# Block transposes on VectorE and swapped key-value sums in a Performer attention and ELU layer kernel

## The chip, the cores and the metric

The kernel runs on one core of one Trainium2 chip. The metric is device time in microseconds (us): the median of three runs of the whole program, one launch, inputs and output in DRAM. Five engines work side by side and meet through semaphores: TensorE (PE; its weight loads are the row PEld), VectorE (DVE), ScalarE (ACT), GpSimd (POOL) and SyncE (SP), which issues all the DMAs.

## The reference

Attention with random features for 8 batches of 8 heads, 576 tokens, head size 64, 128 features; then a two-layer perceptron with ELU over all 4608 tokens.

```python
# q, k, v: (8, 8, 576, 64); omega: (128, 64); m = 128
def phi(x):                                    # x scaled by 64 ** -0.25
    proj = einsum('bhsd,md->bhsm', x, omega)
    h = proj - sum(x * x, -1, keepdims=True) / 2
    return exp(h - max(h, -1, keepdims=True)) / sqrt(m)
q_p, k_p = phi(q_s), phi(k_s)
kv  = einsum('bhsm,bhsd->bhmd', k_p, v)
z   = sum(k_p, axis=2)
num = einsum('bhsm,bhmd->bhsd', q_p, kv)
den = einsum('bhsm,bhm->bhs', q_p, z)[..., None] + 1e-06
x   = (num / den), heads joined                # (4608, 512)
h   = x @ w_in                                 # w_in: (512, 2048), float64
out = elu(h) @ w_out                           # w_out: (2048, 512), float64
```

## The kernel before

**Tiles.** Two heads of a batch make a pair; there are 32 pairs, four to a batch, numbered i = 0 to 31. The 576 tokens of each head are cut into blocks of 128 rows; the last 64 tokens of both heads share a block, so a pair has nine blocks j of 128 tokens by 128 features. Block 2t + a is tile t of head a, and block 8 holds head 0 in rows 0 to 63 and head 1 in rows 64 to 127. The perceptron runs over 12 blocks of 384 tokens, each in 16 steps of 128 hidden units. One step of `layer1` makes 12 matmuls of 384 columns (lines 764 to 766, three for each of four chunks, because every float32 factor is split into a high and a low float32r part), then ELU on ACT and DVE. One step of `layer2` makes nine matmuls of 512 columns (lines 798 to 800) into three accumulators.

**One pair's attention.** `project` makes `hk` and `hq` (line 488 in float32r, line 437 in the first pairs; the exponentials are line 404). `kv` (lines 530 and 535) sums k_p v and the key sums over the nine blocks: the weights are a block of `hk`, 128 by 128, and the moving operand is `v` with a column of ones, 65 columns, in float32. DVE copies the key sums to `z`, ACT copies the rest to `kvf`, features on partitions. `finish` spreads `z` over all partitions with two transposes on PE (`pz`, line 570). DVE multiplies it with q_p and sums to `den` (line 586), takes the reciprocal (595), and POOL or DVE scales q_p by it. PE then transposes the nine blocks of q_p (`pt`, line 607) into three banks, ACT or DVE copies them to `qh`, and four float32 matmuls (`pn`, line 634) multiply by `kvf`: 64 weight columns each, head 0 to partitions 0 to 63 and head 1 to 64 to 127. The result is split into `xh` (helper line 331 or 333) and `xl` (line 647), the input of `layer1`, kept in a ring of two batches.

**What sets the order.** `op` records each operation with engine, cost, due time and buffers; `order` plays the program through by those costs and takes on every engine, among the operations whose inputs and buffers are there, the one due first. The instructions are issued in that order and each engine runs its own list in order. A buffer class (tag) has a fixed number of slots and a line, sorted by due time. The first in line may take a free slot. Another may do so only for the tags in `LOOSE`, `pa` and `h`, and only while two are free. PSUM has eight banks: three of `pa` (projections, `pkv`, `pz`, `pt` and `pn` of pair 4 on), two of `ph` (the output of `layer1`, and `pkv` and `pz` of the first four pairs) and the three accumulators. A pair's due times are its own time less a constant: for pairs 8 on, loads 56.0, k 46.17, `kv` 30.64, q 29.89, the spread 12.0, the transposes 5, `pn` 2 (lines 53 to 68). Steps of `layer1` are due at `step[F]` (from `MLP0 = 58`, `SEG = [8.62, 6.25, 4.29, 5.37, 3.5, 5.81]` for the first six segments of eight steps, then 16 steps a block at `STEP_ATT = 6.59` beside attention or `STEP = 4.91` without; lines 44 to 47), those of `layer2` 3.5 x 4.91 later. Times of a batch come from the stretch of the segment that it runs beside.

Of the kernel before, what the change touches and what calls it, by code (L numbers as in the profile page):

```python
# [18 lines left out]
P = 128  # L19
# [51 lines left out]

NWARM = 7
# [9 lines left out]
class Buf:  # L82


    def __init__(self, pool, shape, dtype, tag, name, n):
        self.args, self.key, self.n = (pool, shape, dtype, name), tag, n
        self.tile, self.left, self.slot, self.listed = None, 0, None, False
# [8 lines left out]
class Plan:  # L96
# [19 lines left out]
    def op(self, eng, ns, due, fn, reads=(), writes=(), nbytes=0, alt=None):  # L116
# [20 lines left out]
        for b in bufs:  # L137
            b.left += 1
        self.tasks.append((engs, due, f, deps, bufs, nbytes))

    def order(self):
# [51 lines left out]
        while len(done) < len(tasks):  # L193
            started = False
            for eng, q in queue.items():
# [3 lines left out]
                for n in q:  # L199
                    engs, due, _, _, bufs, _ = tasks[n]  # L200
                    if ready[n][eng] > now or (best is not None and due >= first):
                        continue
                    if len(engs) > 1 and not mine(n, eng):
                        continue
                    for b in bufs:
                        if b.slot is None:
                            s = sum(z <= now for z in slots[b.key])
                            if s < (1 if line[b.key][-1] is b else 2 if b.key in self.LOOSE else 99):
                                break
                    else:  # L210
                        best, first = n, due
# [70 lines left out]
def performer_elu_kernel(  # L282
# [33 lines left out]

    kvs = [const.tile([P, P], F32, name=f"kvf{i}") for i in range(2)]

# [3 lines left out]
    part = dram.tile([3 * TB, DM], F32, name="part")  # L322
    xh = const.tile([P, NC, RING], F32R, name="xh")
# [196 lines left out]

    def kv(i, due):

        s = st[i]
# [32 lines left out]
        )  # L556

    def finish(i, due):

        s = st[i]  # L560
        h, z = s["hq"], s["z"]
# [6 lines left out]
        def spread():  # L568
            for a in range(2):
                nc.tensor.transpose(pz()[:, a * P:(a + 1) * P], z()[:, a:a + 1].to_broadcast([P, P]), ident)  # L570

        op("PE", 220, due - DUE_Z, spread, (z,), (pz,))
        qh = Buf(sb, [P, 2, S], F32, "qh", f"qh_{i}", 2)
        for g in range(3):
# [27 lines left out]
            )  # L602
            p = bank(i, "pa", f"pt_{i}_{g}")
# [20 lines left out]
            )  # L624
        kvf = kvs[i % 2]
# [12 lines left out]
        for half, (qs, n, p) in enumerate(halves):  # L638
            xs = slice(qs.start + (b % 2) * S, qs.stop + (b % 2) * S)
            key = (b % 2, hp, half)  # L640
            op(
                "ACT", act(n, True), d + 0.8 + half, lambda e, xs=xs, n=n, p=p: copy(e, xh[:, hp, xs], p()[:, 0:n]),
                (p,), (("xh", key),), alt=other("x_hi", "DVE", dve(n)),
# [6 lines left out]
                (p, ("xh", key)), (("xl", key),),  # L650
# [90 lines left out]
    def ring(blk):  # L741
# [3 lines left out]
        for b in range(2):  # L745
            for half, (s0, n) in enumerate(((0, 256), (256, S - 256))):
                if o < b * S + s0 + n and b * S + s0 < o + TB:
                    keys += [(b, hp, half) for hp in range(NHP)]
# [201 lines left out]
```

## Time and profile before

| | |
|---|---|
| three runs | 1087.62 us median (1086.78 to 1089.88) |
| profiled execution, first to last instruction | 1090.7 us; the page gives no other time for it |
| PE busy | 1060.6 us (97%), weight loads 936.8 us (86%) |
| ACT, DVE, POOL busy | 724.7 (66%), 635.9 (58%), 404.4 (37%) |
| DMA | 176.90 MB, 162 GB/s |
| pairs 0 to 7 (unchanged) | attention from 0 to about 150 us |
| pairs 8 to 31 (changed) | from about 260 us, last `pn` at 945 us |

In rows of groups, the numbers after the bar are the time in which at least one of them ran, the mean length of one, and the idle time of the engine before them. Matmuls overlap, so the length of one is no cost: the cost on PE is the distance from its start to the start of the next. A float32 matmul leaves two MATMUL records, a float32r matmul one. In rows of the order of time come start, length, engine, line, operation, output and inputs, tile, shape and how many were merged.

### The profile page before, as it was taken

The page shows a single profiled execution, that of the slowest core. Times are in us where ns is not written, and L with a number is a line of the kernel's source. Part 1 is how long each engine was busy: PE and PEld are TensorE (multiplying, and loading weights), DVE is VectorE, ACT ScalarE, POOL GpSimd, SP SyncE. Part 2 cuts the span into 40 slices and gives each one's busy share as a digit, 9 for nine tenths or more (in the row PEclk, how much of TensorE's full clock was granted, in tenths as well). Part 3 has the DMA queues.
Part 4 walks back from the last instruction along what each step waited for, and adds up shares of the span by engine and source line. Part 5 has one row for each costly group of instructions (what it writes and reads, how often), then busy time and mean ns, then how long its engine had stood idle before and what let it go on. Part 6 is the DMA issues. An engine that isn't in the chain of part 4 may idle for free.

```text
span 1090.7 us, 19072 instructions
## 1 busy us (share of the span) xinstructions
PE 1060.6 (97%) x5971; PEld 936.8 (86%) x5971; DVE 635.9 (58%) x2403; ACT 724.7 (66%) x2027; POOL 404.4 (37%) x372
## 2 busy tenths in 40 slices
PE   7979888999999999999999999999999999999998
PEld 7867777889988888999888888899888888899987
DVE  6788988775776775225676666324566775322221
ACT  6878774546988986337888988326888888432222
POOL 3568746661223343222343233322233342222221
PEclk8889998999999999999999999999999999999999
DMA  7554656656663554434554645434444452343431
GB/s 213 171 181 161 208 188 240 218 186 205 207 205 130 169 170 150 165 118 157 176 155 153 193 139 170 162 119 150 162 155 167 157 164 79 117 164 119 161 121 63
DMA packets 53235, 176.90 MB, mean 162 GB/s; under 512 B 6032, under 2 KB 6224, under 8 KB 53136
## 3 DMA queue, kind: packets, MB, share of 16 engines
q1 hardware_dynamic: 53136, 175.69, 48.4%
q8 instruction: 48, 0.79, 0.3%
q14 instruction: 51, 0.42, 0.1%
HBM read 155.48 MB, written 20.19 MB: 161 GB/s over the span
## 4 chain that ended last, share of the span: by engine, by line
PE 79%; DVE 9%; ACT 6%; issue 3%; DMA 1%; POOL 1%; SPq 0%; DVEq 0%; POOLq 0%; ACTq 0%
PE ph L764 11%; PE acc L798 10%; PE acc L800 10%; PE ph L766 10%; PE acc L799 10%; PE ph L765 10%; PE pkv L535 4%; PE ppq L488 3%; PE pn L634 3%; PE pt L607 2%; PE ppk L488 2%; ACT hk L404 1%; DVE u_w L697 1%; DVE u_w L704 1%; DVE u_w L709 1%
## 5 line engine op out<-in xcount | busy, mean ns | idle before, releaser
L336 POOL TENSOR_TENSOR g<-e,g 128x384 fp32r<-128x384 f32 x182 | 189.2, 1040 | 547.7 <-DVE g L333 405.9
L764 PE MATMUL ph<-xh,w1c 128*128 128x384 f32 x768 | 267.5, 348 | 6.7 <-DVE e L777 6.2
L766 PE MATMUL ph<-xh,w1c 128*128 128x384 f32 x768 | 259.8, 338 | 0.0
L765 PE MATMUL ph<-xl,w1c 128*128 128x384 f32 x768 | 259.7, 338 | 0.0
L777 DVE SCALAR_TENSOR_TENSOR e<-e,ph 128x384 f32<-128x384 f32 x192 | 105.9, 552 | 237.2 <-ACT e L774 232.8
L798 PE MATMUL acc<-w2h,g 128*128 128x512 f32 x576 | 231.4, 402 | 0.0
L773 ACT ACTIVATE e<-ph 128x384 f32<-128x384 f32 x192 | 93.6, 488 | 206.4 <-PE ph L766 198.4
L800 PE MATMUL acc<-w2h,g 128*128 128x512 f32 x576 | 227.7, 395 | 0.0
L799 PE MATMUL acc<-w2l,g 128*128 128x512 f32 x576 | 227.4, 395 | 0.0
L764 PEld LDWEIGHTS ph<-xh,w1c 128*128 128x128 f32 x768 | 145.6, 190 | 20.1 <-DVE e L777 8.5
L765 PEld LDWEIGHTS ph<-xl,w1c 128*128 128x128 f32 x768 | 145.8, 190 | 7.2
L766 PEld LDWEIGHTS ph<-xh,w1c 128*128 128x128 f32 x768 | 145.4, 189 | 0.3 <-POOL w1c L336 0.3
L800 PEld LDWEIGHTS acc<-w2h,g 128*128 128x128 f32 x576 | 108.5, 188 | 25.5
L798 PEld LDWEIGHTS acc<-w2h,g 128*128 128x128 f32 x576 | 108.7, 189 | 15.1 <-issue 2.3
L799 PEld LDWEIGHTS acc<-w2l,g 128*128 128x128 f32 x576 | 108.8, 189 | 12.2
L336 POOL TENSOR_TENSOR hq<-hq,den 128x512 f32<-128x512 f32 (+1 forms) x96 | 90.4, 961 | 36.1 <-DVE den L595 24.6
L774 ACT ACTIVATE e<-e 128x384 f32<-128x384 f32 x192 | 100.7, 525 | 3.1
L333 DVE CAST g<-e 128x384 fp32r<-128x384 f32 x166 | 72.8, 439 | 23.5 <-PE acc L800 18.8
L586 DVE CUSTOM_DVE_ANT_0 junk<-hq,pz 128x128 f32<-128x128 f32 (+1 forms) x320 | 74.1, 279 | 16.9 <-PE pz L570 16.1
L506 DVE CUSTOM_DVE_ANT_0 hq<-ppq,p2q 128x128 f32<-128x128 f32 x216 | 54.3, 287 | 41.8 <-ACT p2q L497 40.2
L506 DVE CUSTOM_DVE_ANT_0 hk<-ppk,p2k 128x128 f32<-128x128 f32 x225 | 56.5, 286 | 36.1 <-ACT p2k L497 34.3
L497 ACT ACTIVATE p2q<-ppq,sqq 128x128 f32<-128x128 f32 x216 | 67.8, 367 | 12.5 <-PE ppq L488 10.8
(82 smaller groups left out, 1620.3 us busy)
## 6 DMA issues: line engine op xcount, KB each, us to landing
w1c<-w1s SPq DMA_DIRECT2D x176, 512.0 KB, 3.3
raw_w<-in_w_dram SPq DMA_DIRECT2D x32, 512.0 KB, 3.6
xk<-in_kx_dram SPq DMA_DIRECT2D x25, 576.0 KB, 3.9
xq<-in_qx_dram SPq DMA_DIRECT2D x24, 576.0 KB, 4.6
v<-in_v_dram SPq DMA_DIRECT2D x32, 325.0 KB, 3.4
out_dram<-o SPq DMA_DIRECT2D x36, 256.0 KB, 2.9
w1s<-w1c SPq DMA_DIRECT2D x16, 512.0 KB, 3.2
xq<-in_q_dram SPq DMA_DIRECT2D x8, 288.0 KB, 4.0
```

What stands on the lines that cost most here:

```text
L336: (nc.vector if e == "DVE" else nc.gpsimd).tensor_tensor(*args)
L506: nc.vector.tensor_tensor_reduce(out=h()[:, j, :], in0=view()[:, a, 0:M], in1=p2()[:, a, :], scale=1.0, scalar=LOWEST, op0=ALU.subtract, o ...
L586: nc.vector.tensor_tensor_reduce(out=junk()[r], in0=h()[r, j, :], in1=pz()[r, a * P:(a + 1) * P], scale=1.0, scalar=EPS, op0=ALU.mult, op1 ...
L764: nc.tensor.matmul(ph(), wh, xh[:, c, o:o + TB], start=(c == 0), stop=False)
L765: nc.tensor.matmul(ph(), wh, xl[:, c, o:o + TB], start=False, stop=False)
L766: nc.tensor.matmul(ph(), wl, xh[:, c, o:o + TB], start=False, stop=(c == NC - 1))
L773: op("ACT", act(TB, True), due, lambda: nc.scalar.activation(e(), ph(), AF.Relu, scale=-1.0), (p,), (e,))
L774: op("ACT", act(TB), due + 0.2, lambda: nc.scalar.activation(e(), e(), AF.Exp, scale=-1.0), (e,), (e,))
L777: lambda: nc.vector.scalar_tensor_tensor(e(), e(), -1.0, ph(), ALU.add, ALU.max), (p, e), (e,),
L798: nc.tensor.matmul(a(), g()[:, 0, ts], w2h[:, f], start=(f == f0), stop=False)
L799: nc.tensor.matmul(a(), g()[:, 0, ts], w2l[:, f], start=False, stop=False)
L800: nc.tensor.matmul(a(), g()[:, 1, ts], w2h[:, f], start=False, stop=(f == f1 - 1))
```

## The change: two other ways through kv and q_p for pairs 8 to 31

For pairs 8 on, `kv_swapped` takes the place of `kv`: `v` is the weight operand (64 columns, one half of the array for each head) and a block of `hk` the moving one (128 columns). The sum comes out transposed, is copied to `kt`, turned by one PE transpose and copied to `kvf`. The key sums no longer come from the ones in `v`: GpSimd adds the blocks of `hk` (five additions), the sum is split in a high and a low part, and `spread` multiplies both by a matrix of ones (two float32r matmuls of 256 columns). `kvf` is written to DRAM and read back in four DMAs, so that each strip of 32 partitions of `zk` holds all 128 features in four groups of columns.

The nine PE transposes and the copies to `qh` go. VectorE's transpose turns each 32 by 32 block of q_p where it stands (block 8 twice), so strip e of `qt` holds the tokens 32e to 32e + 31 of each block, with the features in four groups of columns. `output` then makes 32 float32 matmuls of 160 moving columns: for each feature group j, each strip e and each head a, one on rows 32e to 32e + 31 and half of the columns of the array, each strip into its own bank. They take all three `pa` banks and one `ph` bank at a time. `xh` and `xl` are written from four banks in two pieces each, with strides. `order` gets a rule for operations that need several buffers of one class.

```diff
+NSWAP = 8
+NTURN = 8
...
+        for b in bufs:
+            if b.left == 1:
+                b.need = sum(c.key == b.key and c.left == 1 for c in bufs)
...
+                    need = {}
                     for b in bufs:
                         if b.slot is None:
-                            s = sum(z <= now for z in slots[b.key])
-                            if s < (1 if line[b.key][-1] is b else 2 if b.key in self.LOOSE else 99):
-                                break
+                            need.setdefault(b.key, []).append(b)
+                    for key, bs in need.items():
+                        s = sum(z <= now for z in slots[key])
+                        first_in_line = all(b in bs for b in line[key][-len(bs):])
+                        if s < len(bs) + (0 if first_in_line else line[key][-1].need if key in self.LOOSE else 99):
+                            break
...
+    def replicate(i, due):
+        if i < NTURN:
+            return
+        s, kvf = st[i], kvs[i % 2]
+        zk = s["zk"]
+        op("SP", 500, due + 2.5, lambda: nc.sync.dma_start(kvd[i], kvf), (("kvf", i % 2),), (("kvd", i),), P * P * 4)
+        for e in range(4):
+            op(
+                "SP", 500, due + 3,
+                lambda e=e: nc.sync.dma_start(
+                    zk()[32 * e:32 * e + 32, 4 * M:].rearrange("p (j x) -> p j x", j=4), kvd[i].rearrange("(j c) x -> c j x", j=4)
+                ),
+                (("kvd", i),), ((zk, "kv", e),), P * P * 4,
+            )
+
+    def kv_swapped(i, due):
+        s = st[i]
+        h, v = s["hk"], s["v"]
+        kvf = kvs[i % 2]
+        p = bank(i, "ph", f"pkv_{i}")
+        kt = Buf(sb, [P, P], F32, "kt", f"kt_{i}", 1)
+        def mms():
+            for t in range(-1, 4):
+                for a in range(2):
+                    j, o = (8, 8 * (D + 1) + a * (D + 2)) if t < 0 else (2 * t + a, (2 * t + a) * (D + 1))
+                    nc.tensor.matmul(
+                        p()[a * D:a * D + D, 0:M], v()[:, o:o + D], h()[:, j, :], start=(t < 0), stop=(t == 3)
+                    )
+        parts = parts_of(i, "k")
+        op("PE", 5 * 216, due, mms, [*parts, v], (p,))
+        op(
+            "ACT", act(M, True), due + 1.2, lambda e: copy(e, kt(), p()[:, 0:M]), (p,), (kt,),
+            alt=other("kv", "DVE", dve(M)),
+        )
+        op("PE", 110, due + 1.8, lambda: nc.tensor.transpose(p()[:, M:2 * M], kt(), ident), (kt,), (p,))
+        op(
+            "ACT", act(P, True), due + 2.3, lambda e: copy(e, kvf, p()[:, M:2 * M]), (p,),
+            (("kvf", i % 2),), alt=other("kv", "DVE", dve(P)),
+        )
+        zs = Buf(sb, [P, 2, M], F32, "zs", f"zs_{i}", 1)
+        zk = s["zk"] = Buf(sb, [P, 8 * P], F32, "raw", f"zk_{i}", 3)
...
+        def sums():
+            nc.gpsimd.tensor_tensor(zs(), h()[:, 0:2], h()[:, 2:4], ALU.add)
+            nc.gpsimd.tensor_tensor(zs(), zs(), h()[:, 4:6], ALU.add)
+            nc.gpsimd.tensor_tensor(zs(), zs(), h()[:, 6:8], ALU.add)
+            for a in range(2):
+                r = slice(a * D, a * D + D)
+                nc.gpsimd.tensor_tensor(zs()[r, a], zs()[r, a], h()[r, 8], ALU.add)
...
+        op("POOL", 3 * pool(2 * M) + 2 * pool(M), due + 0.5, sums, parts, (zs,))
+        op("ACT", act(2 * M), due + 3.5, lambda e: copy(e, z(0), flat()), (zs,), ((zk, 0),), alt=other("kv", "DVE", dve(2 * M, True)))
+        op(
+            "POOL", pool(2 * M), due + 4,
+            lambda e: tt(e, z(1), flat(), z(0).bitcast(F32), ALU.subtract), (zs, (zk, 0)), ((zk, 1),),
+            alt=other("g_lo", "DVE", dve(2 * M)),
+        )
+        replicate(i, due)
...
         def spread():
+            if i >= NSWAP:
+                for e in range(2):
+                    nc.tensor.matmul(pz()[:, 0:2 * M], ones, zk()[:, 2 * M * e:2 * M * (e + 1)].bitcast(F32R), start=(e == 0), stop=(e == 1))
+                return
...
-        op("PE", 220, due - DUE_Z, spread, (z,), (pz,))
+        op("PE", 240, due - DUE_Z, spread, ((s["zk"], 0), (s["zk"], 1)) if i >= NSWAP else (s["z"],), (pz,))
...
+            if i >= NTURN:
+                blocks(i, g, h, qt, due - 5 + g)
+                continue
...
+    def blocks(i, g, h, qt, due):
+        n = 4 if g < 2 else 1
+        js = slice(4 * g, 4 * g + n)
+        def turn():
+            for o in range(2 if g == 2 else 1):
+                nc.vector.transpose(
+                    qt()[:, js.start + o:js.stop + o].rearrange("p j x -> p (j x)"),
+                    h()[:, js].rearrange("p j x -> p (j x)"),
+                )
+        op("DVE", (1 if g < 2 else 2) * dve(n * P), due, turn, ((h, "n", g),), ((qt, g),))
+
+    def output(i, qt, due):
+        b, hp = divmod(i, NHP)
+        zk = st[i]["zk"]
+        banks = [Buf(ps, [P, 512], F32, "pa", f"pn_{i}_{e}", 3) for e in range(3)]
+        banks.append(Buf(ps, [P, 512], F32, "ph", f"pn_{i}_3", 2))
+        N = 5 * 32
+        def mms():
+            for j in range(4):
+                for e in range(4):
+                    r, c = slice(32 * e, 32 * e + 32), slice(32 * j, 32 * j + 32)
+                    for a in range(2):
+                        o = slice(a * D, a * D + D)
+                        nc.tensor.matmul(
+                            banks[e]()[o, 0:N], zk()[r, 4 * M + j * P + a * D:4 * M + j * P + a * D + D], qt()[r, a:10:2, c], start=(j == 0), stop=(j == 3)
+                        )
+        op(
+            "PE", 4 * mm(4 * N) + 200, due, mms, [*((qt, g) for g in range(3)), *((zk, "kv", e) for e in range(4))], banks
+        )
...
+        for e, p in enumerate(banks):
+            keys = [(b % 2, hp, half, e) for half in range(2)]
...
+            d = due + 0.8 + 0.4 * e
+            op(
+                "ACT", act(4 * 32, True) + act(32, True), d, high, (p,), [("xh", key) for key in keys],
+                alt=other("x_hi", "DVE", dve(4 * 32) + dve(32)),
+            )
+            op(
+                "DVE", dve(4 * 32) + dve(32), d + 0.4, low, (p, *(("xh", key) for key in keys)),
+                [("xl", key) for key in keys],
+            )
```

More of the change, by code (lines that the diff above doesn't have):

```diff
@@ L521, in kv @@
     def kv(i, due):
+        if i >= NSWAP:
+            kv_swapped(i, due)
+            return
         s = st[i]
@@ L624, in finish @@
             )
+        if i >= NTURN:
+            output(i, qt, due - 2)
+            return
         kvf = kvs[i % 2]
@@ L639, in finish @@
             xs = slice(qs.start + (b % 2) * S, qs.stop + (b % 2) * S)
-            key = (b % 2, hp, half)
+            keys = [(b % 2, hp, half, e) for e in range(4)]
             op(
                 "ACT", act(n, True), d + 0.8 + half, lambda e, xs=xs, n=n, p=p: copy(e, xh[:, hp, xs], p()[:, 0:n]),
-                (p,), (("xh", key),), alt=other("x_hi", "DVE", dve(n)),
+                (p,), [("xh", key) for key in keys], alt=other("x_hi", "DVE", dve(n)),
             )
@@ new lines, in output, with columns, halves, high @@
+    def output(i, qt, due):
[16 more added lines that the diff above has]
+        )
+        x0 = (b % 2) * S
+        def columns(x, e, last):
+            if last:
+                return x[D:P, hp, x0 + 512 + 32 * (e - 2):x0 + 544 + 32 * (e - 2)]
+            v = x[:, hp, x0:x0 + 512].rearrange("p (t e r) -> p e t r", e=4, r=32)[:, e]
+            return v
+        for e, p in enumerate(banks):
+            keys = [(b % 2, hp, half, e) for half in range(2)]
+            def halves(e=e, p=p):
+                yield (lambda x: columns(x, e, False)), p()[:, 0:4 * 32].rearrange("p (t r) -> p t r", r=32)
+                if e < 2:
+                    yield (lambda x: x[0:D, hp, x0 + 512 + 32 * e:x0 + 544 + 32 * e]), p()[0:D, 4 * 32:N]
+                else:
+                    yield (lambda x: columns(x, e, True)), p()[D:P, 4 * 32:N]
+            def high(eng, halves=halves):
+                for dst, src in halves():
+                    copy(eng, dst(xh), src)
+            def low(halves=halves):
+                for dst, src in halves():
+                    nc.vector.tensor_tensor(dst(xl), src, dst(xh).bitcast(F32), ALU.subtract)
+            d = due + 0.8 + 0.4 * e
[6 more added lines that the diff above has]
+                [("xl", key) for key in keys],
@@ L747, in ring @@
                 if o < b * S + s0 + n and b * S + s0 < o + TB:
-                    keys += [(b, hp, half) for hp in range(NHP)]
+                    keys += [(b, hp, half, e) for hp in range(NHP) for e in range(4)]
         return keys
```

26 lines of the change are left out of this document (22 added, 4 removed).

## The prediction

> **What bounds the kernel now.** I read the page first: the summary of the engines and the chain of work that ended last.
>
> ```profile
> span 1090.7 us, 19072 instructions
> PE 1060.6 (97%) x5971; PEld 936.8 (86%) x5971; DVE 635.9 (58%) x2403; ACT 724.7 (66%) x2027; POOL 404.4 (37%) x372
> ...
> PE 79%; DVE 9%; ACT 6%; issue 3%; DMA 1%; POOL 1%; SPq 0%; DVEq 0%; POOLq 0%; ACTq 0%
> ```
>
> PE makes 79% of the chain. A share over the whole span hides stages, so I asked for the busy times of stretches: 260 to 300 us (first changed batch) and 500 to 690 (eight changed pairs).
>
> ```profile
> 260.00:300.00 40.00, 40.00 (x244) 37.40 (x244) 29.67 (x135) 38.48 (x121) 9.45 (x10) 1.00 0.63 210
> ```
>
> ```profile
> core 0: us, PE busy (x) PEld busy (x) DVE busy (x) ACT busy (x) POOL busy (x), PEclk, DMA share, GB/s
> 500.00:690.00 190.00, 189.82 (x1119) 167.97 (x1120) 122.85 (x580) 158.47 (x466) 63.04 (x61) 1.00 0.49 161
> ```
>
> PE never stands still for long where the change is made, at a granted clock of 1.00. So PE time saved there is time saved, as long as no other engine becomes the limit. ACT is next: 158.47 of 190 us, and 38.48 of 40 in the first changed batch, where PE is nonetheless always busy. DVE and POOL have room.
>
> **What the removed work costs on PE.** The cost is the distance between starts, in the order of time around pairs 16 and 18.
>
> ```profile
> 526.61 0.40 PE L488 MATMUL ppq<-om,tq 128*128 128x256 f32 x2
> 526.84 1.00 PE L535 MATMUL pkv<-v,hk 128*128 128x65 f32 x8
> 527.65 0.42 PE L764 MATMUL ph<-xh,w1c 128*128 128x384 f32 x1
> 527.91 0.34 PE L765 MATMUL ph<-xl,w1c 128*128 128x384 f32 x1
> 528.09 0.34 PE L766 MATMUL ph<-xh,w1c 128*128 128x384 f32 x1
> 528.26 0.60 PE L607 MATMUL pt<-ident,hq 128*128 128x128 f32 x4
> 528.62 0.48 PE L488 MATMUL ppq<-om,tq 128*128 128x256 f32 x2
> 528.94 0.27 PE L607 MATMUL pt<-ident,hq 128*128 128x128 f32 x1
> 528.97 0.48 PE L798 MATMUL acc<-w2h,g 128*128 128x512 f32 x1
> 529.28 0.40 PE L799 MATMUL acc<-w2l,g 128*128 128x512 f32 x1
> ...
> 530.91 0.39 PE L799 MATMUL acc<-w2l,g 128*128 128x512 f32 x1
> 531.14 0.40 PE L800 MATMUL acc<-w2h,g 128*128 128x512 f32 x1
> 531.47 1.19 PE L634 MATMUL pn<-qh,kvf 128*64 128x256 f32 x8
> 532.59 0.50 PE L488 MATMUL ppq<-om,tq 128*128 128x256 f32 x2
> 532.93 0.34 PE L764 MATMUL ph<-xh,w1c 128*128 128x384 f32 x1
> ```
>
> ```profile
> 588.90 0.39 PE L570 MATMUL pz<-ident,z 128*128 128x128 f32 x2
> 589.04 0.48 PE L798 MATMUL acc<-w2h,g 128*128 128x512 f32 x1
> 589.36 0.39 PE L799 MATMUL acc<-w2l,g 128*128 128x512 f32 x1
> ```
>
> The undisturbed distances are 0.23 for 512 columns (530.91 to 531.14), 0.18 for 384 (527.91 to 528.09), 0.23 for two of 256 (526.61 to 526.84).
>
> - `pkv`: eight records take 0.81 (526.84 to 527.65), and the matmul behind them 0.26 instead of 0.18: 0.89 a half, 1.78 for both. Line 530 adds two records of the same kind, estimated at a quarter of eight, 0.20: 1.98 us a pair.
> - `pt`: four take 0.36 and delay the two behind them by 0.09 (0.32 for 0.23): 0.45. One alone takes 0.03 and 0.08 behind it: 0.11. A pair: 1.01 us.
> - `pz`: 0.14, and 0.09 behind it: 0.23 us.
> - `pn`: it starts 0.33 after the last 512-column matmul, 0.10 late; takes 1.12; delays the next by 0.11 (0.34 for 0.23): 1.33 us.
>
> Together 4.55 us of PE a pair.
>
> **What the new work costs on PE.** The question is how many tiles of the array run at once. The same start of `pn`, asked for in two short windows:
>
> ```profile
> 531.47 0.44 PE L634 MATMUL pn<-qh,kvf 128*64 128x256 f32 x2
> ...
> 531.47 0.65 PE L634 MATMUL pn<-qh,kvf 128*64 128x256 f32 x4
> ```
>
> The windows end at 531.60 and 531.80. Each float32 matmul leaves two records, the second of which needs the same half of the array as the first and adds to the same output. Two records had started by 531.60 and ended within 0.44 us of the first start, so I read them as the first records of head 0 and of head 1, the two halves running together. If a record streams its columns twice, one of 256 columns takes a little less than the 0.23 of 512, say 0.21, and one of 320 takes 0.27; 4 rounds of two halves, two of each length, make 0.96, which with 0.16 of loading and ending gives the 1.12.
>
> - `kv_swapped`: ten matmuls, 20 records, 10 rounds of two halves; 128 columns in two passes are half of 0.21: 1.07, plus 0.16, plus 0.10 before and 0.11 behind: 1.44. The transpose of `kt` is one like the single `pt`: 0.11.
> - `spread`: two float32r matmuls of 256 columns: 0.23.
> - `output`: 32 matmuls, 64 records, on eight tiles (four strips, two halves). Strips appear nowhere in this trace. Lower bound: all eight run together, 8 rounds of 160 columns in two passes (0.21 x 160/256 = 0.13): 1.07, with the same 0.16, 0.10 and 0.11: 1.44 us. Middle: only the two halves overlap, 32 rounds: 4.2 + 0.37 = 4.57 us. Upper: the records come one by one at the pace of the transposes (0.36 for four): 64 x 0.09 = 5.8 + 0.2 = 6.0 us.
>
> I take 1.5 for `output`, next to the lower bound: the halves' start shows tiles of one array taken independently, and the strips write to different banks and read different partitions. Sum 1.44 + 0.11 + 0.23 + 1.5 = 3.28 us, so 1.27 us less a pair, and over 24 pairs 30 us.
>
> The Trainium skill speaks against this: TensorE: Matmul & The Clock Gate, Part 3, says that matmuls start and end strictly in program order, only weight loads being pulled ahead. By that rule a tile's second record would hold back the next tile's first, `output` would cost about the middle bound and the kernel would lose; the two records started together in `pn` disagree with it. The same page (Wait — 56ns) gives a floor of some 25 ns between starts: 64 of them are 1.6 us, `output` would be about 2.0, and by that the sum falls by 12 us less; the two starts of `pn` disagree for two tiles, and no run here shows eight.
>
> **The other engines.** These rows price the moved work.
>
> ```profile
> L331 ACT COPY qh<-pt 128x512 f32<-128x512 f32 x64 | 37.6, 589 | 30.5 <-PE pt L607 30.0
> L331 ACT COPY qh<-pt 128x128 f32<-128x128 f32 x32 | 8.8, 276 | 0.4 <-PE pt L607 0.4
> L331 ACT CAST xh<-pn 128x320 fp32r<-128x320 f32 x32 | 14.1, 441 | 1.0 <-PE pn L634 1.0
> L331 ACT CAST xh<-pn 128x256 fp32r<-128x256 f32 x32 | 11.9, 373 | 8.0 <-PE pn L634 8.0
> L647 DVE TENSOR_TENSOR xl<-pn,xh 128x320 fp32r<-128x320 f32 x32 | 15.5, 485 | 1.5 <-ACT xh L331 1.5
> L647 DVE TENSOR_TENSOR xl<-pn,xh 128x256 fp32r<-128x256 f32 x32 | 13.5, 422 | 22.1 <-ACT xh L331 21.9
> L445 DVE TENSOR_REDUCE mxq<-ppq 128x4 f32<-128x512 f32 x16 | 10.9, 681 | 1.1 <-PE ppq L437 1.0
> L333 DVE COPY kvf<-pkv 128x128 f32<-128x128 f32 x4 | 1.1, 280 | 0.0
> L336 POOL TENSOR_TENSOR g<-e,g 128x384 fp32r<-128x384 f32 x182 | 189.2, 1040 | 547.7 <-DVE g L333 405.9
> L336 POOL TENSOR_TENSOR hq<-hq,den 128x128 f32<-128x128 f32 x32 | 18.0, 563 | 0.0
> ```
>
> ACT loses the copies to `qh` (2 x 0.59 + 0.28 = 1.45) and the two casts to `xh` (0.81). It gains eight smaller casts (four of 128 columns at 0.28, four of 32 at some 0.2: 1.9), `kt` 0.28 and the high part of the sums 0.37. Net +0.3. DVE gains the block transposes: two of 512 columns and two of 128. For 512 columns the bounds are the 0.49 that 320 columns take in `xl` and 1.36, the 512-column reduction passed twice; I take that reduction once, 0.68, and for 128 columns the copy's 0.28: 1.9. The `xl` pieces add 8 at 0.28 and 0.2 less 0.91: +1.0. Together +2.9 a pair. POOL gains three sums and a difference of 256 columns (between 0.56 and 1.04: 0.8 each) and two sums of 128 (0.56): 4.3.
>
> For eight pairs in 500 to 690, shortened by 10 to 180 us: ACT 158.47 + 2.4 = 161, 89%; DVE 122.85 + 23 = 146, 81%; POOL 63 + 34 = 97, 54%. None reaches PE. I cost these at nothing on the path, since PE was full beside an ACT at 38.48 of 40; but the queues get longer, so I charge 10 us in all: 0.2 us a pair for the wait for four banks, and 5 us for the first changed batch and the last pair of each batch, where the next block waits for `xh`.
>
> **DMAs and queues.** Five DMAs more a pair go on SP, one writing `kvf` and four reading it after it has landed.
>
> ```profile
> w1c<-w1s SPq DMA_DIRECT2D x176, 512.0 KB, 3.3
> ...
> w1s<-w1c SPq DMA_DIRECT2D x16, 512.0 KB, 3.2
> ```
>
> SP stands at the first read until the write has landed, at most the 3.2 us of the larger write. Behind it stand the next `w1c` load, loads of later pairs and stores of results. A `w1c` load may start when its buffer comes free, two steps before use; a step is 12 x 0.175 + 9 x 0.23 = 4.2 us of PE at least (384 columns lie between 0.17 and 0.18), so 8.4 less 3.3 for landing leaves 5.1, more than 3.2. `output` is due 28.6 us after `kv`, and the replication takes some 7 with both landings. Without that cover it would cost up to 3 us a pair.
>
> **The sum.** On the profiled execution: 1090.7 - 30 + 10 = 1071. This span is 3.1 us above the median of the runs, so by the median 1087.6 - 20 = **1067 us**.
>
> **The rivals.**
>
> *Strips one after another (slower).* Place: PE, inside `output`. Price: 4.57 instead of 1.5, so 1.8 us lost a pair instead of 1.27 won: 1087.6 + 24 x 1.8 + 10 = about 1140. It decides from 2.8 us for `output`, where gain and cost cancel. For it: no strip is in the trace, and PE takes its instructions from one list. Against it: the halves in `pn`. Chance 0.14. (The Trainium skill's rule on program order, above, would end here.)
>
> *The line of the banks holds up PE (slower).* `ph` is served strictly by due time, and until now was `layer1`'s alone. Now `output` of pair i stands in that line, so a step due later cannot start before it, and it needs three free `pa` banks too.
>
> ```profile
> L764 PE MATMUL ph<-xh,w1c x336: 331/337/691, 55.1 to 527.7; 128*128 128x384 f32 x168
> ...
> L764 PE MATMUL ph<-xh,w1c x173: 332/337/691, 55.1 to 310.2; 128*128 128x384 f32 x173
> ```
>
> At four records a step, 84 steps had begun before `pn` of pair 16 (first row) and 44 before that of pair 8 (second). By the constants, `pn` of pair 16 is due at 536.1 and 84 steps are due before it, so the two already run in lockstep; for pair 8 (due 290.9) it is 42 steps, so two would now have to wait, 8.4 us of PE work. Elsewhere `layer2`, some two steps behind, covers about 4 us of waiting. If that cover failed and PE idled 2 us a pair while projections clear the banks, the change would cost 48 - 30 + 8 = 26: about 1114. It decides from 1.3 us a pair. Chance 0.12.
>
> *The gain is eaten (no change).* ACT and DVE in-order queues, or strips started at a pace of about 40 ns (`output` near 2.6): 30 shrinks to 5 or so against 5 to 10 of waits, 1080 to 1092, most likely 1087. Chance 0.14.
>
> *The strips work and PE stays the bound:* 0.60, with 1053 to 1079 as its own range.
>
> **How the numbers follow.** What this kernel's measurement can tell from no change is about 0.3%, 3.3 us. Faster: 0.60, and a third of the eaten case, together 0.64. Same: 0.08. Slower: 0.14 + 0.12 and the rest of the eaten case, 0.28. The time is that of the likeliest case, 1067. The low end is full concurrency with no waits, 30 us and a little from shorter DVE work: 1053. The high end takes in the bank case, 1114, and leaves out the serial strips.
>
> **What would show it.** Right: the 64 records of `output` start within about 1.2 us; no rows of `pt`; PE busy all through 260 to 920; ACT near 89% and DVE near 81% in the stretch of eight pairs; the last `output` some 20 us before 945. Wrong: `output` over 2.8 us; idle PE before `output` that ends on a bank's reader; `layer1` waiting behind it; block transposes of 512 columns near 1.2 us; POOL sums delaying `g`, so that `layer2` waits.

## The result, and the profile after

| | median | range | ratio to before, 95% interval |
|---|---|---|---|
| before, same call | 1088.79 us | 1086.78 to 1091.10 | |
| changed | 1081.42 us | 1078.57 to 1084.06, and one of 3878.48 | 0.9912 [0.9893, 0.9932] |
| changed, second call | 1084.49 us | 1082.51 to 1085.38 | 0.9947 [0.9926, 0.9967] |
| changed, third call | 1084.44 us | 1083.26 to 1086.62 | 0.9943 [0.9926, 0.9959] |

The change is faster by 0.5 to 0.9%, about 7 us; 20 were forecast. In the first call the profiled execution took 3878 us (matmuls of 512 columns start 0.84 us apart there, not 0.23), so the profile below is that of the second call. From its page, the engines and the chain:

```profile
span 1080.7 us, 22409 instructions
...
PE 1034.6 (96%) x7171; PEld 909.6 (84%) x7171; DVE 712.8 (66%) x2656; ACT 718.9 (67%) x2140; POOL 481.9 (45%) x488
...
PE 74%; DVE 13%; ACT 4%; DMA 3%; issue 3%; POOL 2%; SPq 0%; DVEq 0%; POOLq 0%; ACTq 0%
```

PE works 26 us less and the span is only 10 us shorter. DVE's part of the chain rose from 9% to 13%, PE's fell from 79% to 74%. The two stretches that the prediction used (columns as there):

```profile
core 0: us, PE busy (x) PEld busy (x) DVE busy (x) ACT busy (x) POOL busy (x), PEclk, DMA share, GB/s
260.00:300.00 40.00, 39.66 (x244) 35.20 (x243) 29.90 (x130) 35.92 (x115) 15.81 (x19) 1.00 0.69 222
500.00:690.00 190.00, 187.65 (x1554) 164.88 (x1553) 150.13 (x663) 161.60 (x517) 88.06 (x100) 1.00 0.57 181
```

DVE stands at 150.13 of 190 us (79%, forecast 81%), ACT at 161.60 (85%, forecast 89%), POOL at 88.06 (46%, forecast 54%). PE, which missed 0.18 us of this stretch before, now misses 2.35. The strips in order of time:

```profile
557.00 0.40 PE L978 MATMUL acc<-w2h,g 128*128 128x512 f32 x1
557.32 1.37 PE L788 MATMUL pn<-qt,zk 32*64 32x160 f32 x64
558.62 0.44 PE L942 MATMUL ph<-xh,w1c 128*128 128x384 f32 x1
558.90 0.34 PE L943 MATMUL ph<-xl,w1c 128*128 128x384 f32 x1
```

All 64 records start within the 1.30 us from the first to the next matmul; the product starts 0.09 late behind a 512-column matmul (0.32 for 0.23) and delays the next by 0.10 (0.28 for 0.18). Its cost is 1.49 us, and 1.5 was forecast. In 16 of the 24 pairs it is 1.30 us to the next matmul as here, in the others 1.33 to 2.10. Asked for in a window that ends at 557.37, the product shows eight records, one for each tile:

```profile
557.32 0.39 PE L788 MATMUL pn<-qt,zk 32*64 32x160 f32 x8
```

The moved work, in groups between 240 and 945 us:

```profile
L767 DVE STREAM_TRANSPOSE qt<-hq 128x512 f32<-128x512 f32 x48 | 33.5, 701 | 1.1 <-POOL hq L353 0.6
L819 DVE TENSOR_TENSOR xl<-pn,xh 128x128 fp32r<-128x128 f32 x96 | 27.2, 284 | 18.2 <-ACT xh L348 17.7
L593 POOL TENSOR_TENSOR zs<-zs,hk 64x128 f32<-64x128 f32 x46 | 25.4, 553 | 3.1
...
L588 POOL TENSOR_TENSOR zs<-hk 128x256 f32<-128x256 f32 x23 | 20.3, 883 | 0.0
...
L819 DVE TENSOR_TENSOR xl<-pn,xh 64x32 fp32r<-64x32 f32 x96 | 17.6, 183 | 0.7
...
L767 DVE STREAM_TRANSPOSE qt<-hq 128x128 f32<-128x128 f32 x48 | 11.5, 278 | 0.3 <-POOL hq L353 0.3
```

The prices of the prediction hold here too: 0.70 for a block transpose of 512 columns (0.68), 0.28 for 128 (0.28), 0.88 and 0.55 for the sums (0.8 and 0.56).

**Where the time went.** The start of a given step of `layer1` (record 4F + 1 of its first line) is the same piece of work in every kernel, so its time is a milestone. Step 24 lies behind the first eight pairs, 24 to 64 beside the first changed batches, 64 to 112 and 112 to 160 beside the next two pairs of batches.

| start of step, us | 24 | 64 | 112 | 160 | 184 |
|---|---|---|---|---|---|
| before | 213.6 | 438.7 | 693.5 | 949.1 | 1047.2 |
| changed (second call) | 219.3 | 443.5 | 691.4 | 939.1 | 1037.1 |
| changed less before | +5.7 | +4.8 | -2.1 | -10.0 | -10.1 |

The table is of one execution each, and its last entry is some 3 us more than the runs give. By it 5.7 us are lost in the eight pairs that the change was not meant to touch, the first changed stretch wins 0.9 where eight pairs at 1.27 should win 10, and each later stretch wins 7 to 8. The rest of this document takes these three apart.

### The profile page after: what moved, and what is told of

The parts are those of the page before. It is cut to its first block, busy times and chain, and to the rows that moved or that the text cites. A ratio compares the mean times of both kernels' runs of the same rounds, so it can differ in the third digit from the quotient of the medians.

```text
span 3876.7 us, 22409 instructions
## 1 busy us (share of the span) xinstructions
PE 3870.9 (100%) x7171; PEld 2610.8 (67%) x7171; DVE 685.0 (18%) x2656; ACT 746.9 (19%) x2140; POOL 465.7 (12%) x488
## 4 chain that ended last, share of the span: by engine, by line
PE 100%; ACT 0%; POOL 0%; issue 0%; POOLq 0%
PE ph L942 13%; PE ph L943 13%; PE ph L944 13%; PE acc L976 13%; PE acc L977 13%; PE acc L978 13%; PE pn L788 3%; PE ppq L454 3%; PE pkv L566 3%; PE ppk L505 3%; PE ppq L505 2%; PE ppk L454 2%; PE pkv L624 2%; PE pn L741 1%; PE pt L711 1%; PE pz L665 1%
## 5 line engine op out<-in xcount | busy, mean ns | idle before, releaser
L942 PE MATMUL ph<-xh,w1c 128*128 128x384 f32 x768 | 733.0, 954 | 0.0
L943 PE MATMUL ph<-xl,w1c 128*128 128x384 f32 x768 | 731.2, 952 | 0.0
L944 PE MATMUL ph<-xh,w1c 128*128 128x384 f32 x768 | 730.3, 951 | 0.0
L976 PE MATMUL acc<-w2h,g 128*128 128x512 f32 x576 | 677.6, 1176 | 0.0
L977 PE MATMUL acc<-w2l,g 128*128 128x512 f32 x576 | 670.2, 1163 | 0.0
L978 PE MATMUL acc<-w2h,g 128*128 128x512 f32 x576 | 666.4, 1157 | 0.0
L942 PEld LDWEIGHTS ph<-xh,w1c 128*128 128x128 f32 x768 | 376.2, 490 | 176.9 <-issue 156.3
L943 PEld LDWEIGHTS ph<-xl,w1c 128*128 128x128 f32 x768 | 390.1, 508 | 141.2 <-issue 127.8
L944 PEld LDWEIGHTS ph<-xh,w1c 128*128 128x128 f32 x768 | 384.6, 501 | 118.0 <-issue 94.7
L978 PEld LDWEIGHTS acc<-w2h,g 128*128 128x128 f32 x576 | 277.0, 481 | 221.1 <-issue 217.3
L976 PEld LDWEIGHTS acc<-w2h,g 128*128 128x128 f32 x576 | 280.0, 486 | 166.5 <-issue 156.2
L977 PEld LDWEIGHTS acc<-w2l,g 128*128 128x128 f32 x576 | 286.2, 497 | 143.1 <-issue 136.0
L505 PEld LDWEIGHTS ppk<-om,tk 128*128 128x128 f32 x225 | 98.2, 454 | 52.1 <-issue 43.5
L505 PE MATMUL ppk<-om,tk 128*128 128x256 f32 x225 | 126.3, 709 | 0.0
```

Of the source, the lines that this page charges most:

```text
L505: nc.tensor.matmul(p()[:, a * 256:(a + 1) * 256], y()[:, o:o + P], om, start=True, stop=True)
L942: nc.tensor.matmul(ph(), wh, xh[:, c, o:o + TB], start=(c == 0), stop=False)
L943: nc.tensor.matmul(ph(), wh, xl[:, c, o:o + TB], start=False, stop=False)
L944: nc.tensor.matmul(ph(), wl, xh[:, c, o:o + TB], start=False, stop=(c == NC - 1))
L976: nc.tensor.matmul(a(), g()[:, 0, ts], w2h[:, f], start=(f == f0), stop=False)
L977: nc.tensor.matmul(a(), g()[:, 0, ts], w2l[:, f], start=False, stop=False)
```

## The experiments

Each call ran the kernel before beside it; ratios are to that. The first entry is the changed kernel once more, for its profile:

> The changed kernel once more, for a profile of an undisturbed execution. Time 1077 to 1084 us. Theory A (strips all at once, the rest of the forecast gain lost in waits of PE): the 64 records of the strips' matmuls start within about 1.2 us, 1.5 us of PE a pair with both ends, and PE stands idle or waits some 20 us more in all than before. Theory B (strips start at a pace): first record to the next matmul 1.7 to 2.2 us, some 2.0 of PE a pair, the saving is then 0.8 us a pair, 19 us, and waits are about the 10 us that the prediction charged.

Measured: 1084.49 us, 0.9947, read above.

**One part at a time.** In `swap_only` (`NTURN = 32`) only `kv_swapped` and the sums on GpSimd are done from pair 8 on; in `turn_only` (`NSWAP = 32`, `zk` made beside the old `kv`) only the block transposes and the strips.

> From pair 8 on only the swapped sum of k_p v and the key sums on GpSimd; q_p is turned on PE and multiplied as before. Both theories give the sum 1.44 + 0.11 us of PE in place of 1.98, so 0.43 us a pair, 10 us: 1078 to 1081 us if it goes straight into the time. If it stays within 3 us of before, the GpSimd sums or the second visit to the bank give it back.

> From pair 8 on only the block transposes on VectorE and the product by strips; the sum of k_p v and the key sums as before. Theory A: 1.5 us of PE in place of 1.01 + 1.33, 0.84 a pair, 20 us less PE work, of which 20 us of waits eat nearly all: 1082 to 1090. Theory B: 2.0 in place of 2.34, 0.34 a pair, 8 us, less some waits: 1080 to 1088. The two differ in the profile: the distance from the strips' first start to the next matmul, about 1.2 or about 1.9 us.

Measured: 1101.39 us, ratio 1.0112 [1.0081, 1.0142], and 1088.99 us, 0.9982 [0.9964, 1.0001]. Both are behind the whole change, and step 24 starts at 219.0 and 215.1 us in them, 5.4 and 1.5 later than before, though no pair before 8 does anything new. That pointed at the planner.

**The planner alone.** `rule_only` takes neither way (`NSWAP = NTURN = 32`): left are the new rule of `order`, the price 240 of the spread and the tile of ones. `old_rule` is the changed kernel with the old rule wherever no operation that needs three or more banks is first in line, and the old price for the first pairs:

```diff
-                        if s < len(bs) + (0 if first_in_line else line[key][-1].need if key in self.LOOSE else 99):
+                        if len(bs) < 3 and line[key][-1].need < 3:
+                            short = any(s < (1 if line[key][-1] is b else 2 if key in self.LOOSE else 99) for b in bs)
+                        else:
+                            short = s < len(bs) + (0 if first_in_line else line[key][-1].need if key in self.LOOSE else 99)
+                        if short:
                             break
...
-        op("PE", 240, due - DUE_Z, spread, ...
+        op("PE", 240 if i >= NSWAP else 220, due - DUE_Z, spread, ...
```

PE's matmuls in the trace are then those of before up to the first swapped product of pair 8, 1330 records; in the changed kernel they depart after 236, at 43 us, where the first projection of pair 4, which takes a `pa` bank, is put off.

> No pair is changed; only the planner's new rule for several buffers, the new cost 240 of the spread, and the constant of ones stay. PE's list differs from before's from its 41st row on, in pairs 2 to 7. Theory (the new rule costs time in the unchanged pairs): layer 1's step 24 comes some 4 to 6 us later than before, 219 instead of 214 us, and the end is 1092 to 1096. Rival (the late step 24 of the changed kernel came from the clock or from chance): within 3 us of before.

> The changed kernel, with the planner's old rule and old cost wherever no operation with three buffers of a class is first in line: PE's list is that of before up to the first changed operation of pair 8. Theory: 5 to 6 us faster than the changed kernel, 1073 to 1079. Rival: the same as the changed kernel within 3 us.

Measured: `rule_only` 1097.68 us, 1.0062 [1.0041, 1.0083]; `old_rule` 1077.01 us, 0.9874 [0.9859, 0.9888]. The rule and the price alone make the kernel slower, by more than the 1092 to 1096 us expected: `rule_only` starts the five steps of the table 7.2, 6.8, 7.6, 7.2 and 7.2 us after before, so the whole loss is there by step 24. Without them the change wins 13.5 us. The rule and the price were not run apart. A repetition of three kernels on one chip:

> The changed kernel a third time, beside the next two on one chip: 0.991 to 0.995 of before, about 1083 us.

> The kernel with the old rule a second time. If the planner's new rule and price cost 7 us in the first eight pairs, the ratio to before lies 0.004 to 0.007 below that of the changed kernel of this call; if the first comparison was an accident of two chips, the two ratios are within 0.002 of each other.

Measured: changed 1084.44 us, 0.9943 [0.9926, 0.9959]; old rule 1077.46 us, 0.9880 [0.9859, 0.9902]. The difference, 0.6% or 7 us, is there again. The first 200 us of before, of the changed kernel and of the one with the old rule, in two stretches each:

```profile
0.00:100.00 100.00, 86.25 (x547) 73.47 (x548) 78.42 (x237) 76.72 (x230) 57.56 (x53) 0.90 0.58 180
100.00:200.00 100.00, 89.36 (x487) 76.78 (x486) 83.53 (x209) 70.14 (x180) 63.45 (x50) 0.97 0.61 208
```

```profile
0.00:100.00 100.00, 81.86 (x547) 70.13 (x548) 80.30 (x235) 75.87 (x228) 59.20 (x53) 0.90 0.57 176
100.00:200.00 100.00, 86.44 (x457) 73.57 (x456) 81.78 (x216) 64.43 (x169) 63.54 (x52) 0.93 0.61 203
```

```profile
0.00:100.00 100.00, 85.39 (x556) 72.69 (x556) 79.78 (x253) 78.40 (x236) 59.94 (x55) 0.90 0.61 184
100.00:200.00 100.00, 87.91 (x478) 75.71 (x479) 82.04 (x198) 67.99 (x174) 62.90 (x51) 0.97 0.60 204
```

In the changed kernel PE is busy 168.3 us of the first 200, before 175.6, with the old rule 173.3; the granted clock between 100 and 200 is 0.93, 0.97 and 0.97. So up to some 4 us of the loss (an estimate, 0.04 of 100 us) may come by way of the clock. `turn_only`, whose matmuls come in the order of the changed kernel up to pair 8, has 0.97 there too and starts step 24 at 215.1 us, not 219.3: one execution's time of step 24 is good to a few us. In the six profiles with the new rule it is 215.1 to 221.7, in the twelve with the old one, before among them, 210.0 to 215.3.

Under the new rule another operation may take a bank only while as many stay free as the first in line needs. That is meant for the strips, but the old `pn` needs two `pa` banks, so a projection out of turn now has to find three free where two were enough; the one put off at 43 us is of this kind. From step 24 on the changed kernel and the one with the old rule run alike: the latter starts the five steps at 213.1, 437.6, 685.5, 933.2 and 1031.2 us, wins 0.6, 6.9 and 7.9 in the three stretches, and the former 0.9, 6.9 and 7.9.

**The line of the `ph` banks.** With the old rule, a step of `layer1` due later may take a `ph` bank while a strips' product is first in that line and two are free.

```diff
+                            loose = key in self.LOOSE or key == "ph" and line[key][-1].args[3].startswith("pn_")
-                            short = any(s < (1 if line[key][-1] is b else 2 if key in self.LOOSE else 99) for b in bs)
+                            short = any(s < (1 if line[key][-1] is b else 2 if loose else 99) for b in bs)
```

> As old_rule, and a later step of layer 1 may take a bank of the class ph while the strips' product is first in its line, if two are free. Theory (the strict line costs the waits at 336 to 348 us in the first changed batch and the 8 us by which step 48 is late): step 48 comes 5 us or more earlier than in old_rule, the end is 3 to 6 us earlier, 1068 to 1075. Rival (the product itself is late because VectorE is late, and the line only passes this on): steps move, the end does not, within 2 us of old_rule.

Measured: 1077.89 us, 0.9884 [0.9869, 0.9898], no different from 0.9874. Step 56 starts 2 us earlier than with the old rule alone, and step 112 1.4 us later: what the line costs in the first changed batch is given back. Step 48 comes 3.2 us earlier; 5 or more were expected if the line held the gain. The line is not what holds it.

**One part at a time, with the old rule.**

> Old rule in the planner, kv_swapped and GpSimd's key sums from the third batch on, the old PE transposes and the old output (NTURN = 32); PE's list is that of before up to the first changed operation of pair 8. Theory A (the rule and the parts simply add up): the part alone was 1.0112 of before, the rule alone 1.0062, so here 1.005, about 1094 us. Theory B (the part alone lost only through what the rule did to the list, there and behind it): PE's own work falls by 45.6 - 31.2 for the products, less 0.7 for the transpose of kt and 2.3 for the spread, 11 us in 24 pairs, and with some 5 us of waits the time is 1082 to 1086, 0.993 to 0.996.

> Old rule in the planner (the new one only where an operation with three banks or more is first), block transposes and strips from the third batch on, the old kv (NSWAP = 32). Theory A (parts add up): 0.9982 less 0.0062, so 0.992, about 1081 us. PE's own work falls by 19.6 for the transposes and rises by 33.5 - 25.8 for the products: 12 us; with no new waits it would be 1078, 0.989. If the two parts' gains with the old rule (this and the swap alone) add to less than the 13.5 us of both together, they help each other.

Measured: the swap alone 1099.38 us, 1.0064 [1.0043, 1.0085]; transposes and strips alone 1083.12 us, 0.9909 [0.9885, 0.9933]. Each part does add to the rule (theory A forecast 1.005 and 0.992), and theory B, that PE's saved work would show, fails for the swap. But the parts do not add to each other: alone one loses 0.6% and the other wins 0.9%, together they win 1.2 to 1.3%. On top of the strips the swap thus seems to win another 0.3% (0.9909 to 0.9874; the intervals meet). PE's waits with the swap alone, between 240 and 930 us (us in all, times, longest):

```profile
PE pt L715 <- POOL hq L357: 3.3, 6, 0.9
PE ppq L509 <- DVE mxq L527: 2.3, 5, 0.7
PE ppq L509 <- DVE den L691: 2.1, 3, 0.7
PE ph L946 <- DVE e L959: 2.0, 2, 1.1
```

The first row names a link that the kernel before has too, with 0.4 us: PE's transposes of q_p stand in its list right behind POOL's scaling of q_p, but here POOL also does 3.6 us of sums a pair. With block transposes it is DVE that waits for POOL, and PE goes on. The row is 3.3 of the 13 us that PE stands idle in these 690; what makes the rest of the 13 to 17 us between 1099.4 and theory B's 1082 to 1086 was not tried.

**GpSimd's sums.** In the next two kernels the last four of five additions are left out. `sums_cut` is the changed kernel and has a lower price in the planner too, so its order may move; in `old_rule_sums` the price stays, so that PE, ACT and DVE keep their lists.

```diff
-            nc.gpsimd.tensor_tensor(zs(), zs(), h()[:, 4:6], ALU.add)
-            nc.gpsimd.tensor_tensor(zs(), zs(), h()[:, 6:8], ALU.add)
-            for a in range(2):
-                r = slice(a * D, a * D + D)
-                nc.gpsimd.tensor_tensor(zs()[r, a], zs()[r, a], h()[r, 8], ALU.add)
```

> The changed kernel with only the first of GpSimd's five additions of the key sums; the other four are left out, so the denominators lack most keys. That takes 2.7 us a pair from GpSimd and nothing from PE. Theory S (the sums hold up GpSimd and, through operands in the shared memory, VectorE, and PE waits for them): 5 to 10 us faster than the changed kernel, 1071 to 1077. Rival (VectorE's own new work, transposes and more pieces, is what PE waits for): within 3 us of the changed kernel.

> The kernel with the old rule, with only the first of GpSimd's five key-sum additions (the denominators leave out most keys), and with the planner's cost as it was: the lists of PE, ACT and DVE are the same, row by row. GpSimd's work falls by 3.0 us a pair. If the sums stand behind nothing: 1076 to 1078. If they delay GpSimd's share of g, for which layer2 then waits: 1070 to 1074.

Measured: 1080.76 us, 0.9911 [0.9894, 0.9928], against 0.9912, 0.9947 and 0.9943 of the changed kernel in its three calls; and 1073.73 us, 0.9833 [0.9812, 0.9855], against 0.9874 and 0.9880. With the lists kept, taking some 2.7 us a pair from POOL (two sums of 0.8 and two of 0.55), 65 in all, wins 3 to 5 us: a small part of the rest.

**VectorE's load.** `old_rule_twice` does every block transpose twice (`for o in (0, 0, 1, 1) if g == 2 else (0, 0)`), `old_rule_low` leaves out the low halves of the 128-column pieces. Neither moves a row of another engine's list.

> The kernel with the old rule, every block transpose done twice (same output, same order of all lists): DVE's work rises by 0.70 + 0.70 + 0.28 + 0.28 = 1.96 us a pair, 47 us in all. If DVE's transposes are hidden behind PE: 1077 to 1080. If they stand ahead of the maxima (mxq) that free the pa banks of the projections, so that PE's waits behind kv and the projections (some 13 us in the kernel with the old rule) come from them: 1085 to 1100.

> The kernel with the old rule, in which the low halves xl of the 128-column pieces are not written from the third batch on (they keep the values of an earlier batch, so the result lacks a correction); the 32-column pieces remain, and the lists of PE, ACT and POOL are the same, row by row. DVE's work falls by 4 x 0.284 = 1.14 us a pair, 27 us in all. If DVE's load still costs at the rate that doubling the transposes showed (42 us for 47 us of work, 0.9): 1053 or so. If the cover had just been used up and the first microseconds are nearly free: 1070 to 1077, 0 to 0.25 us for each us taken away.

Measured: 1119.09 us, 1.0245 [1.0223, 1.0267], and 1077.15 us, 0.9888 [0.9864, 0.9913]. 47 us more of DVE cost 42, more than the 8 to 23 expected; 27 us less win nothing. The stretch of eight pairs, with the old rule and with doubled transposes:

```profile
500.00:690.00 190.00, 187.67 (x1549) 165.11 (x1544) 149.09 (x662) 160.47 (x513) 84.88 (x95) 1.00 0.56 178
```

```profile
500.00:690.00 190.00, 181.75 (x1386) 158.30 (x1386) 150.49 (x644) 155.49 (x493) 81.95 (x93) 0.99 0.54 169
```

DVE's share hardly rises, 149.09 to 150.49 of 190: the kernel slows down around it at 79%. PE is busy 662.00 us between 240 and 930, against 679.94 with the old rule, at a granted clock of 0.97 to 0.98 for 0.99 to 1.00. The idle fifth of DVE is not free for any work: its list has places where PE waits for one result. Such a place in the changed kernel, PE and then DVE:

```profile
573.77 1.31 PE L566 MATMUL pkv<-hk,v 128*64 128x128 f32 x20
575.01 0.50 PE L505 MATMUL ppq<-om,tq 128*128 128x256 f32 x2
...
576.40 0.27 PE L576 MATMUL pkv<-ident,kt 128*128 128x128 f32 x1
577.99 0.36 PE L505 MATMUL ppq<-om,tq 128*128 128x256 f32 x1 [1.31 <-DVE mxq L523]
```

```profile
575.49 0.73 DVE L353 TENSOR_TENSOR hq<-hq,den 128x128 f32<-128x128 f32 x1
576.14 0.70 DVE L767 STREAM_TRANSPOSE qt<-hq 128x512 f32<-128x512 f32 x1
576.87 0.55 DVE L955 SCALAR_TENSOR_TENSOR e<-e,ph 128x384 f32<-128x384 f32 x1
577.34 0.28 DVE L523 CUSTOM_DVE_ANT_0 hq<-ppq,p2q 128x128 f32<-128x128 f32 x1
577.54 0.08 DVE L523 DVE_READ_ACCUMULATOR2_ANT mxq<- 128x1 f32 x1
577.54 0.29 DVE L523 CUSTOM_DVE_ANT_0 hq<-ppq,p2q 128x128 f32<-128x128 f32 x1
```

The projections of 575.01 fill a `pa` bank that the maxima `mxq` clear; a scaling and a transpose of another pair and a step of ELU stand ahead of these on DVE, and PE waits 1.31 us for the bank. The low halves lie behind `xh`, off this path: without them these waits are the same 5.7 us in 7.

**Places and prices.** `old_rule_costs` gives the planner the measured prices of the new operations. `old_rule_late` makes the block transposes due 2.5 us later (`due - 2.5 + g` for `due - 5 + g`), behind the maxima where both are ready; `late_2` is the same kernel beside the repetition above.

> The kernel with the old rule, with the planner's prices of the new operations as the traces measured them: products of kv 1.30 us for 1.08, key sums 3.63 for 2.58, their difference 0.78 for 0.64, block transposes 0.70 for 0.60 and 0.56 for 0.40, the strips' product 1.41 for 1.28, low halves 0.47 for 0.30. If part of the 13 us of waits comes from a list planned with prices too low, 1070 to 1075. If the waits come from how full DVE and ACT are around each pair, whatever the order: 1075 to 1079, no difference.

> The kernel with the old rule, with the block transposes due 2.5 us later in the planner, so that on DVE's list they stand behind the maxima of the projections where both are ready. In the trace of the kernel with the old rule a 512-column transpose of 0.70 us stands between the projection and its maximum at the places where PE waits for a bank (5.7 us in 7 waits between 240 and 930). If these waits are the transposes' doing: 1068 to 1073, and the waits of the projections on the maxima shrink below 2 us. If what counts is only how full the stretch is, the waits move elsewhere (to the product, which then waits for qt): 1075 to 1083.

> The kernel with the old rule and later block transposes a second time. If their place on VectorE's list matters, the ratio is 0.003 below that of the kernel with the old rule, as the two calls gave it (0.9841 and 0.9874); if that was the chips, the two are within 0.0015.

Measured: right prices 1083.06 us, 0.9938 [0.9916, 0.9959], slower than the wrong ones by 6 us; later transposes 0.9841 [0.9826, 0.9856] and then, beside the kernel with the old rule on one chip, 0.9881 [0.9861, 0.9901] against its 0.9880. The waits on `mxq` fall from 5.7 us in 7 to 4.2 in 6, not below 2, and one of 2.2 before the strips is new: moved, not won. Both orders change hundreds of rows, so a difference of 6 us from an order is as much as any single part of the rest here, and no price below that can be read from a run that reorders the list. That holds for the parts alone as well, and for why the planner's rule costs what it does: that the rule and the price cost 7 us is measured twice, which of the moved operations costs them is not.

## Why the prediction was right and wrong

**PE's work: right.** The strips at 1.49 us for 1.5 and the moved operations of DVE and POOL are shown above, with the shares of the engines, of which POOL's alone is far off (46% for 54%). The swapped product takes 1.24 us to the next start (573.77 to 575.01 in the order of time) for 1.23 without its delays. With the old rule PE's starts from first to last cover 15.9 us less than before; PE's steps between starts beyond those of undisturbed matmuls of their kind grow by some 10 us from step 24 to the last strips, and a lower clock near 345 us (below) adds about 1.4. So some 27 us of work were saved (an estimate), and 30 were forecast.

**"The change starts at pair 8": the step that failed.** The forecast gave no term to the pairs before, though `order`'s new rule and the price 240 stand in the diff and hold for every pair. It was read as a rule for the strips; the old `pn` with its two `pa` banks falls under it as well. What the runs show in place of nothing: 7 us between the changed kernel and the one with the old rule (5.7 at step 24 in the profiles), about half the miss of 13 us.

**The waits: too small, and in part of another kind.** 10 us were charged: 0.2 a pair for the wait for four banks, and 5 for the first batch and for `xh` at the ends of batches. By the stretches, eight pairs at 1.27 should win 10.2, and with the old rule they won 0.6, 6.9 and 7.9, so 9.6, 3.3 and 2.3 were missing, some 15 us; 3 of these are work that was not saved, so the waits are some 12. PE is idle 10.1 us between 240 and 930 with the old rule, 1.4 before. The first batch is where the most is lost, as charged. But no row of PE's waits ends on `xh`, and the strips have one row, of 0.3 us. In their place, between 240 and 930:

```profile
PE ppq L509 <- DVE mxq L527: 5.7, 7, 1.3
PE acc L980 <- ACT g L352: 1.9, 1, 1.9
PE acc L982 <- POOL g L357: 1.5, 4, 0.8
```

The largest single place is in the first stretch, with the old rule: PE, then ACT, then the chain, then the granted clock.

```profile
340.63 0.50 PE L980 MATMUL acc<-w2h,g 128*128 128x512 f32 x1 [1.88 <-ACT g L352]
342.18 0.50 PE L982 MATMUL acc<-w2h,g 128*128 128x512 f32 x1 [0.81 <-POOL g L357]
```

```profile
338.63 1.55 ACT L425 ACTIVATE hk<-hk,nbk 128x128 f32<-128x128 f32 x5
340.09 0.49 ACT L352 CAST g<-e 128x384 fp32r<-128x384 f32 x1
```

```profile
338.25 2.40 POOL hq L357 x3
340.65 0.01 issue
340.66 1.47 POOL g L357
342.13 0.04 issue
342.18 0.50 PE acc L982
```

```profile
338.00:344.00 6.00, 3.31 (x49) 2.15 (x54) 4.25 (x16) 2.56 (x9) 5.76 (x8) 0.88 0.45 168
340.00:342.00 2.00, 0.73 (x2) 0.30 (x2) 1.96 (x4) 0.58 (x2) 1.99 (x3) 1.00 0.00 0
342.00:344.00 2.00, 1.82 (x43) 1.58 (x50) 0.39 (x3) 0.00 (x0) 1.84 (x4) 0.63 0.78 272
344.00:346.00 2.00, 2.00 (x38) 1.56 (x23) 0.58 (x4) 0.93 (x6) 1.33 (x3) 0.51 0.06 23
346.00:348.00 2.00, 2.00 (x22) 1.75 (x22) 1.47 (x6) 1.44 (x4) 0.74 (x1) 1.00 0.00 0
```

ACT makes the high part of the `g` that `layer2` needs behind five exponentials, and PE's first gap, 1.88 us, ends on it. POOL scales three parts of q_p before it makes the low part, and the second gap ends there. POOL was free at 340.65, but it reads the high part too, which came at 340.58: neither place alone made this wait. PE stands for 2.7 of 6 us and then runs at a clock of 0.63 and 0.51 for two stretches of 2 us. The changed kernel has the same place 6 us later. The prediction's cover for ACT and POOL was their share of the stretch; what failed was the place of their work in the list.

**The rivals.** Strips one after another: wrong, 1.30 us for 64 records. The Trainium skill's rule of strict program order (TensorE: Matmul & The Clock Gate, Part 3), from which the prediction drew the rival of slow strips, does not make them slow: the same section describes packed tiles as starting some 4 ns apart, and here eight start between 557.32 and 557.37 us. (The prediction also set the two starts of `pn` against a floor of 25 ns; its lines show them within 0.13 us, too coarse for that. The eight here are not.) The line of the banks: not the cause (`old_rule_ph`), though the first changed batch is where the most is lost. The gain eaten: in part, the time lies at its edge, but not by the slow strips that it named; the in-order queue of DVE that it named is there.

**Other engines at nothing: not so.** PE's waits on the maxima grew from 0.3 us before to 5.7. DVE was called room, and at 79% it had none ahead of the maxima: the next 1.96 us a pair cost 0.9 us for each microsecond. Behind them it had, as the low halves show. How much of the waits is DVE's first 2.9 us a pair stays open; cutting the transposes themselves was not tried.

**The best version** that does the whole work is the changed kernel with the old rule: 1077.0 and 1077.5 us, 0.9874 and 0.9880. With later transposes it is as fast, 1076.9 and 1078.6 us.

## What to carry to other kernels

A change to the planner is a change to everything that it plans: before any price is worked out, compare the order of the engines up to the first operation that was meant to move. An engine's share of a stretch is no measure of what it can still take; look for the results in its list on which the bounding engine waits, and price what is put ahead of them. A gain in work on the bounding engine is a ceiling: here some 27 us of it became 13 with the order kept, and 7 with it disturbed.

## What the runs showed of the hardware

- Eight tiles of 32 rows by 64 columns run together: 64 float32 records of 160 columns take 1.30 us up to the next matmul, 20 ns each in the mean, and the first eight start within 0.05 us. This is less than the floor of about 25 ns that the Trainium skill gives for starts (TensorE: Matmul & The Clock Gate, Wait — 56ns), which stands there for matmuls back to back, not for tiles.
- A wait can be paid twice. After the 2.7 us above, the granted clock falls to 0.63 and 0.51 in two stretches of 2 us and is 1.00 again, where the kernel before shows 1.00 all through: half speed for some 3.4 us, an estimate from these two. The Trainium skill (the same page, Part 1) ties a lower clock to an idle window of about 3.4 us; here two gaps of 1.9 and 0.8 us, with two matmuls between them, sufficed.
- Turning 32 by 32 blocks of float32 on VectorE takes 701 ns for 128 by 512 and 278 for 128 by 128, about the 681 of a reduction over 512 columns and the 280 of a copy of 128 in the kernel before.
